# Polysketch attention and a noisy top-2 router on one core: reordering the head, summing early sketches in PSUM, and storing the last tiles together

## The chip, the cores and the metric

One core of a Trainium2 chip runs the whole kernel in one launch. The metric is device time in microseconds (us), the median of three runs: 346.47 before the change (346.46 to 346.67). Engines: PE is TensorE, DVE VectorE, ACT ScalarE, POOL GpSimd, SP SyncE. DMA transfers are issued by SP, ACT and POOL; "SPq" and "ACTq" in the profile are the issuing instructions.

## What is computed

Attention with sketched polynomial features for B=4 batches, H=4 heads, S=1088 positions, DH=32, R=8; its output, 4352 tokens of D=128, goes through a mixture of E=8 experts (F=1024) of which a noisy router takes two per token:

```python
def phi(x):                                   # R*R = 64 features per head
    a = einsum('rd,bhsd->bhsr', S1, x)
    b = einsum('rd,bhsd->bhsr', S2, x)
    return einsum('bhsi,bhsj->bhsij', a, b).reshape(..., 64)
q_p, k_p = phi(q), phi(k)
kv  = einsum('bhsf,bhsd->bhfd', k_p, v);  z = k_p.sum(axis=2)
attn = einsum('bhsf,bhfd->bhsd', q_p, kv) / (einsum('bhsf,bhf->bhs', q_p, z) + 1e-6)
x = attn.transpose(0, 2, 1, 3).reshape(4352, 128)
noisy = x @ w_gate + log1p(exp(x @ w_noise)) * noise
top2 of noisy per token, weights = softmax over the two
out[token] = sum over its two experts e of weight * (relu(x @ w1[e]) @ w2[e])
```

All inputs and the output are float32.

## The kernel before

**Planning.** No engine's order is written out by hand. Every piece of work is a job in a `Plan` with an engine (or a choice of two), an estimated cost, a priority (lower is sooner), what it reads and writes, and the rotating buffers it opens. The planner lists the jobs in time on its own cost figures; each engine then executes its instructions in exactly the planned order, waiting on semaphores where data come from another engine. A change in a cost or a priority can so move instructions that it does not mention.

**Head, batch 0.** A token tile is 128 positions; a batch has eight and a half tile. SP loads the sketch words, keys, values and queries. The sketch words are split into a high and a low part `s` (`split`, L555), turned by PE (L535/536) and copied by DVE to `sk` (L541), a matrix of 128 x 128 whose column halves are the high and the low part, so that the features are a sum of two products. `turned` (L583) transposes keys and queries on DVE (kT, qT). `features` (L595) multiplies a tile's kT or qT by `sk` in one matmul of 128 columns (L606), leaving the high and the low result side by side in PSUM; ACT or DVE copies the low half out (`lo`, L322), DVE adds it to the high half (`ab`, L614), and another DVE product (L628) makes the 64 features (phk, phq). `keys_values` (L636) then sums features times values over all tiles (L669; `vaug` is the values with a column of ones, four copies by ACT or POOL), folds the router's weights into the result (L690) and copies it to `kvw` in two halves by partitions, one for each pair of heads. `queries` turns phq (L717), multiplies it by kvw (L728), and divides (den, L757/758; lh L745), which gives the logits `lg` (L747).

**Router, `router`.** ACT makes softplus parts u, sp; POOL makes a (L869, L870) from the logits and multiplies by the noise (L873 to L875); DVE makes `noisy` (L888), top, the gates g, the mask mk; PE counts the places of a token in its expert (L934, L937), and pos, gm follow. The noise is one SP load (136 KB) into a buffer `x`, laid out by six small POOL copies (L400). POOL also makes, at the kernel's start, constants for later: the padding block `pad` (L488/489), the limits `reach` and `capt` (L494/496), token numbers `pid` (L500 to L507), which are copied to the gather records `xg` (L984).

**Experts.** The first blocks (u=0 to 3) are gathered straight from SBUF: `block` builds four one-hot matrices `o` (DVE compare, L1054; the fourth by ACT as Abs and Relu, L1047/1050), PE multiplies them with the tokens (L1060), ACT copies to bT, PE runs hp (L1108), ACT relu (L1116), PE acc (L1123). Later blocks come through DRAM: POOL scatters tokens with indirect DMAs (L809), SP loads xb. Results go to `pairs` in DRAM by POOL's scatters; `sums` loads both results of each token (pr), DVE adds them (L1179) and SP or ACT stores the tiles. While PE has nothing to do in the first 30 us, `idle` puts in filler matmuls on zeros (L1435).

**Early work.** Four q tiles of batch 0 (4 to 7) and four k tiles of batch 1 (0 to 3) have their features matmuls before the router (`early`, PSUM tag acc); their lo copies on ACT and adds on DVE come behind it, as the one-hots' data (`gone`) tell.

**Tail.** The last blocks do not go through `pairs`: `to_tokens` (L1255) multiplies their results by one-hots of the tokens and sums them in three PSUM banks `totals`, one for tiles (0,1), one for the half tile (4), one for tiles (2,3), in this order. `sums` adds each to the pair sum (L1186), and ACT issues three stores: tiles (0,1), the half tile, tiles (2,3).

## Time and profile before

| | us |
|---|---|
| median of three runs | 346.47 |
| profiled execution: its own time | 347.08 |
| profiled execution: span from the first to the last instruction | 345.1 |
| PE busy in the span | 336.2 (97%) |
| POOL, DVE, ACT busy | 232.1, 146.4, 136.4 |
| first expert matmul (L1108) starts | 27.47 |
| last pair of L1255 begins / last total (L1186) begins | 338.50 / 339.25 |

Times inside the execution are counted from the span's start. A row of a timeline gives start, length, engine, line, operation, out<-in and how many instructions were put together; the brackets hold the idle time of the engine before it and what ended it. A row of the chain of waits gives start, length, engine, tile and line. A row of waits gives who waited for whom, total, count and longest. The mean granted clock of PE was 0.994 of full speed.

### The profile page before, as it was taken

To read this page: it belongs to the slowest core of one execution; us is meant where nothing else is said; L and a number is where in the kernel's file an instruction comes from. 1 tells how busy PE (TensorE), PEld (TensorE's weight loads), DVE (VectorE), ACT (ScalarE), POOL (GpSimd) and SP (SyncE) were. 2 spreads that over 40 slices of the span, in tenths; PEclk is the share of its full clock that TensorE was granted. 3 is DMA by queue.
4 is the path that set the end of the run, shared out by engine and by line. 5 is a ranking of instruction groups with operands and counts; after the bars stand their busy time and mean duration, and the time that the engine had idled before them with its cause. 6 is when DMAs were issued, how large, how long until landed. Compare 5 with 4: busy or idle time off the path is not lost.

```text
span 345.1 us, 7493 instructions
## 1 busy us (share of the span) xinstructions
PE 336.2 (97%) x2585; PEld 313.9 (91%) x2586; DVE 146.4 (42%) x547; ACT 136.4 (40%) x305; POOL 232.1 (67%) x385
## 2 busy tenths in 40 slices
PE   8999999999999999999999999999999999999992
PEld 3859999999999999999999999999999999999992
DVE  5889794877636688555862000020102000112101
ACT  2357542543531445323334333433334333434430
POOL 8854868896899857898968889878334433354410
PEclk9999999999999999999999999999999999999997
DMA  7999839144571376511353213365125211114421
GB/s 217 327 346 268 288 63 356 60 116 114 139 221 39 62 187 133 138 40 39 74 74 71 54 43 54 69 184 120 37 36 185 67 32 27 29 32 166 147 77 39
DMA packets 68922, 41.17 MB, mean 119 GB/s; under 512 B 49877, under 2 KB 61078, under 8 KB 68880
## 3 DMA queue, kind: packets, MB, share of 16 engines
q1 hardware_dynamic: 63360, 30.93, 35.1%
q0 software_dynamic: 4704, 9.15, 8.2%
q10 hardware_dynamic: 816, 0.58, 0.6%
q8 instruction: 21, 0.34, 0.4%
q14 instruction: 21, 0.17, 0.2%
HBM read 24.18 MB, written 16.65 MB: 118 GB/s over the span
## 4 chain that ended last, share of the span: by engine, by line
PE 95%; DVE 2%; ACT 1%; issue 1%; POOL 0%; DVEq 0%; ACTq 0%; POOLq 0%
PE acc L1123 37%; PE hp L1108 37%; PE bank L606 5%; PE bank L728 4%; PE bank L669 4%; PE bank L717 2%; PE hp L1435 1%; PE acc L669 1%; PE bank L1255 1%; PE turn L1060 1%; PE bank L690 0%; ACT o L1050 0%; PE bank L937 0%; DVE lg L747 0%; ACT o L1047 0%
## 5 line engine op out<-in xcount | busy, mean ns | idle before, releaser
L1123 PEld LDWEIGHTS acc<-w2s,h 128*128 128x128 f32 x1152 | 145.8, 192 | 4.6
L1123 PE MATMUL acc<-w2s,h 128*128 128x128 f32 x1152 | 149.8, 275 | 0.0
L1108 PE MATMUL hp<-bT,w1s 128*128 128x128 f32 (+1 forms) x768 | 147.3, 328 | 0.2 <-ACT bT L322 0.2
L1116 ACT ACTIVATE h<-hp 128x512 f32<-128x512 f32 x144 | 86.0, 597 | 123.2 <-PE hp L1108 122.9
L1108 PEld LDWEIGHTS hp<-bT,w1s 128*128 128x128 f32 x768 | 111.6, 191 | 6.4 <-ACT h L1116 0.5
L809 POOL DMA_INDIRECT pairs<-y,ix x66 | 65.1, 986 | 66.1 <-ACT y L322 55.9
L809 POOL DMA_INDIRECT xs<-xg,to x72 | 73.0, 1014 | 19.2 <-issue 9.1
L808 POOL MEMSET zb<- 128x400 bf16 (+1 forms) x142 | 63.1, 444 | 0.2 <-PE hp L1435 0.2
L1096 DVE STREAM_TRANSPOSE bT<-xb 128x256 f32<-128x256 f32 (+1 forms) x40 | 15.6, 390 | 101.9 <-PE hp L1108 89.8
L322 ACT COPY y<-acc 128x128 f32<-128x128 f32 (+1 forms) x48 | 15.3, 320 | 28.1 <-PE acc L1123 27.6
L1179 DVE TENSOR_TENSOR o<-pr 128x512 f32<-128x512 f32 (+2 forms) x13 | 6.7, 525 | 36.1 <-DMA pr<-pairs 36.1
L728 PE MATMUL bank<-kvw,pT 128*128 128x98 f32 x144 | 18.2, 274 | 0.0
L728 PEld LDWEIGHTS bank<-kvw,pT 128*128 128x128 f32 x144 | 17.4, 192 | 0.6 <-DVE kvw L322 0.3
L669 PE MATMUL bank<-phk,vaug 128*128 128x128 f32 (+1 forms) x108 | 13.1, 277 | 0.0
L322 ACT COPY lo<-bank 128x256 f32<-128x256 f32 (+3 forms) x20 | 6.5, 328 | 16.5 <-PE bank L606 16.5
L322 ACT COPY pT<-bank 128x512 f32<-128x512 f32 (+1 forms) x16 | 8.8, 559 | 10.6 <-PE bank L717 9.1
L669 PEld LDWEIGHTS bank<-phk,vaug 128*128 128x128 f32 (+1 forms) x108 | 12.5, 191 | 0.4
L614 DVE TENSOR_TENSOR ab<-bank,lo 128x256 f32<-128x256 f32 (+3 forms) x20 | 7.2, 360 | 12.5 <-ACT lo L322 12.4
L628 DVE TENSOR_TENSOR phk<-ab 128x512 f32<-128x512 f32 (+1 forms) x20 | 12.2, 629 | 0.4
L628 DVE TENSOR_TENSOR phq<-ab 128x512 f32<-128x512 f32 (+1 forms) x20 | 11.8, 628 | 0.2
L991 DVE TENSOR_TENSOR xg<-x,g 128x512 f32<-128x512 f32 (+1 forms) x16 | 11.2, 750 | 0.0
L1435 PE MATMUL hp<-zb 128*128 128x512 bf16 x29 | 9.5, 463 | 1.6 <-DVE zb L439 1.3
(177 smaller groups left out, 243.7 us busy)
## 6 DMA issues: line engine op xcount, KB each, us to landing
xs<-pad SPq DMA_DIRECT2D x9, 516.0 KB
w1s<-in_moe_w_dram SPq DMA_DIRECT2D x8, 512.0 KB
w2s<-in_moe_w_dram SPq DMA_DIRECT2D x8, 512.0 KB
pr<-pairs SPq DMA_DIRECT2D x7, 512.0 KB
xb<-xs SPq DMA_DIRECT2D x96, 32.0 KB
kq<-in_k_dram SPq DMA_DIRECT2D x4, 544.0 KB
kq<-in_q_dram SPq DMA_DIRECT2D x4, 544.0 KB
vld<-in_v_dram SPq DMA_DIRECT2D x14, 128.0 KB
```

The source lines that it names most:

```text
L322: paces.append(A.copy(o, i) if e == "ACT" else V.tensor_copy(o, i))
L606: T.matmul(ps.t[rows, 2 * W * i:2 * W * i + 2 * W], lhsT=lhsT, rhs=sk[:].rearrange("p c h x -> p (c h x)"), start=True, stop=True)
L628: V.tensor_tensor(out=jobs[i][2].t[rows, jobs[i][1]:jobs[m - 1][1] + 1, :, :].rearrange("p c h (i j) -> p (c h) i j", i=R), in0=factors(i, ...
L669: T.matmul(kvp.t[:, P * a:P * a + P], lhsT=va.t[0:K, t, hs, :].rearrange("p h d -> p (h d)"), rhs=pk.t[0:K, t, hs, :].rearrange("p h f -> ...
L728: T.matmul(ps2.t[:, c0:c0 + 2 * YW], lhsT=pT.t[:, P * (2 * i + a):P * (2 * i + a) + P], rhs=kvw.t[:, a, :], start=True, stop=True)
L808: G.memset(zb[:, 0:FIRST_SPACER if kind == "first" else SPACER], 0.0)
L809: ins = G.indirect_dma_start(**kw)
L1096: add("DVE", vec(P * n), lambda _: V.transpose(bT.t[:, 0:P * n], flat()), r=[xb], w=[bT], prio=TOP + u)
L1108: T.matmul(hp.t[:, P * n * i:P * n * (i + 1)], lhsT=w1s[:, e, P * (js * g + i):P * (js * g + i + 1)], rhs=bT.t[:, 0:P * n], start=True, st ...
L1116: paces.append(A.activation(out=h.t[:], in_=hp.t[:], func=AF.Relu))
L1123: T.matmul(acc.t[:, D * c:D * c + D], lhsT=h.t[:, P * (n * i + c):P * (n * i + c + 1)], rhs=w2s[:, e, j, :], start=(j == 0 and c == 0), st ...
L1435: ins = T.matmul(warm()[:], lhsT=zb[:, 0:P], rhs=zb[:], start=True, stop=True)
```

## The change

In words, in the order of the diff:

1. `lo` is gone as a buffer; the low half is copied into `ab` (four buffers instead of two) and added in place.
2. Head keys: the first transpose (tiles 0, 1) gets priority -51, ahead of `sk` on DVE; the other key transposes follow at 0.5, 0.9 and 1.9, so that the four features groups of the keys stand together.
3. The value copies of the head get priority 2.05 and a POOL cost of 0.45; POOL's jobs of priority 13 and more (pad, limits, token numbers) depend on them. In the planned order POOL makes three of the four copies (two before), then wg, pad, the first limits, the noise copies, and only then the token numbers.
4. The two early features groups are `summed`: per tile two matmuls of 64 columns (high, then low) accumulate in the same PSUM columns, and one ACT copy behind the router's `sp` brings the sum to `ab`.
5. The two halves of `kvw` in the head are written by ACT and DVE, declared apart so that neither waits for the other; the early key transposes of batch 1 wait for both.
6. The fourth one-hot of block 0 is a DVE compare like the other three; blocks 1 to 3 keep ACT, at a cost of 0.45.
7. The tail: the last batch's four tiles are one piece with two loads and two pair sums; the totals lie in two banks, the half tile in one, both pairs of tiles in the other; PE's order is (4), (0,1), (2,3); SP stores the half tile and ACT all four tiles in one store.

```diff
     tag("qT", 1, [P, S])
-    tag("lo", 2, [P, 4, 2 * R * H])
-    tag("ab", 2, [P, 4 * H, 2, R])
+    tag("ab", 4, [P, 4 * H, 2, R])
     tag("kvT", 2, [P, 2, R * R])
...
             paces.append(A.copy(o, i) if e == "ACT" else V.tensor_copy(o, i))
+            return paces[-1]
...
     def pool_job(cost, prio, emit, w, r=()):
-        add("POOL", cost, lambda e: emit(), r=r, w=w, prio=prio)
+        job = add("POOL", cost, lambda e: emit(), r=r, w=w, prio=prio)
+        if prio >= 13:
+            behind_values.append(job)
+    behind_values = []
...
-    def features(jobs, prio, after=(), first=None, early=None):
+    def features(jobs, prio, after=(), first=None, early=None, summed=False):
...
                 lhsT = xT.t[:, P * t:min(P * t + P, S)]
+                if summed:
+                    for c in range(2):
+                        T.matmul(ps.t[rows, W * i:W * i + W], lhsT=lhsT, rhs=sk[:, c, :, :].rearrange("p h x -> p (h x)"),
+                                 start=(c == 0), stop=(c == 1))
+                    continue
                 T.matmul(ps.t[rows, 2 * W * i:2 * W * i + 2 * W], lhsT=lhsT,
                          rhs=sk[:].rearrange("p c h x -> p (c h x)"), start=True, stop=True)
-        last = (add if early is None else plan.add)("PE", n * mm(128), emit, lat=0.15, r=["sk"] + [(xT, t) for xT, t, _ in jobs],
+        last = (add if early is None else plan.add)("PE", n * (2 * mm(64) if summed else mm(128)), emit, lat=0.15, r=["sk"] + [(xT, t) for xT, t, _ in jobs],
                    w=[ps], prio=prio if first is None else first, touch=[dst for _, _, dst in jobs], after=after if early is None else (early,))
-        lo, ab = new("lo"), new("ab")
-        gone = [] if early is None else [onehot["pos"], onehot["gm"]]
+        ab = new("ab")
+        flat = lambda: ab.t[rows, 0:n * H, :, :].rearrange("p (i h) w r -> p i (h w r)", h=H)
         x4 = lambda: ps.t[rows, 0:2 * W * n].rearrange("p (i c y) -> p i c y", i=n, c=2)
-        add(EV, either(W * n), lambda e: copy(e, lo.t[rows, 0:n, :], x4()[:, :, 1, :]), r=[ps] + gone, w=[lo], prio=prio)
-        add("DVE", vec(W * n), lambda e: V.tensor_tensor(
-            out=ab.t[rows, 0:n * H, :, :].rearrange("p (i h) w r -> p i (h w r)", h=H),
-            in0=x4()[:, :, 0, :], in1=lo.t[rows, 0:n, :], op=ALU.add), r=[ps, lo], w=[ab], prio=prio if early is None else 12.95 if jobs[0][2] is kv_of[0][1] else 13.2)
+        if summed:
+            add("ACT", act(W * n), lambda e: copy(e, ab.t[rows, 0:n * H, :, :].rearrange("p x w r -> p (x w r)"), ps.t[rows, 0:W * n]),
+                r=[ps], w=[ab], prio=prio if early is None else 12, after=() if early is None else (onehot["sp"],))
+        else:
+            add(EV, either(W * n), lambda e: copy(e, flat(), x4()[:, :, 1, :]), r=[ps], w=[ab], prio=prio)
+            add("DVE", vec(W * n), lambda e: V.tensor_tensor(out=flat(), in0=x4()[:, :, 0, :], in1=flat(), op=ALU.add), r=[ps], w=[ab],
+                prio=prio)
...
     kv_of, behind_first, freed = {}, [], []
-    behind_gates = []
+    behind_gates, folded_first = [], []
...
         for h in range(H):
-            add(("ACT", "POOL") if head else "ACT", {"ACT": act(256), "POOL": 0.4} if head else act(256), lambda e, h=h: copy(e, va.t[:, 0:C, h, 0:DH], vld.t[:, h, 0:C, :]),
-                r=["ones_v"] + [(vld, l) for l in range(4)], w=[(va, h)], prio=prio + 2.2, after=hold)
+            value = add(("ACT", "POOL") if head else "ACT", {"ACT": act(256), "POOL": 0.45} if head else act(256),
+                        lambda e, h=h: copy(e, va.t[:, 0:C, h, 0:DH], vld.t[:, h, 0:C, :]),
+                        r=["ones_v"] + [(vld, l) for l in range(4)], w=[(va, h)], prio=prio + (2.05 if head else 2.2), after=hold)
+            if head:
+                for job in behind_values:
+                    job.deps.add(value)
         add("ACT", act(128), lambda e: A.copy(va.t[0:HB, C, :, 0:DH], vld.t[0:HB, :, C, :]),
...
             if early is not None and i == 0:
-                turned(kT, kld, c0, c1, 22, True)
-                features([(kT, t, pk) for t in range(c0, c1)], prio + i + 1, after, 21.5, early)
+                turned(kT, kld, c0, c1, 22, True).deps.update(folded_first)
+                features([(kT, t, pk) for t in range(c0, c1)], prio + i + 1, after, 21.5, early, True)
                 continue
-            freed.append(turned(kT, kld, c0, c1, prio + i))
+            freed.append(turned(kT, kld, c0, c1, (-51, 0.5, 0.9)[i] if head else prio + i))
             features([(kT, t, pk) for t in range(c0, c1)], prio + i + 1, after)
-        freed.append(turned(kT, kld, 8, 9, prio + 1))
+        freed.append(turned(kT, kld, 8, 9, prio + (1.9 if head else 1)))
         turned(qT, qld, 8, 9, prio + (25 if head else 2))
...
         for l in range(2):
-            add(EV, either(98), lambda e, l=l: copy(
-                e, kvw.t[64 * l:64 * l + 64, :, YW * l:YW * l + YW],
-                ps.t[64 * l:64 * l + 64, 0:2 * YW].rearrange("p (a y) -> p a y", a=2)),
-                r=[ps, "kvw0"], w=[(kvw, l)], prio=prio + 3)
+            def half(e, l=l):
+                ins = copy(e, kvw.t[64 * l:64 * l + 64, :, YW * l:YW * l + YW],
+                           ps.t[64 * l:64 * l + 64, 0:2 * YW].rearrange("p (a y) -> p a y", a=2))
+                if head:
+                    apart(ins, "kvw")
+                    wrote(ins, "kvw")
+            done = add(("ACT", "DVE")[l] if head else EV, 0.25 if head else either(98), half, r=[ps, "kvw0"], w=[(kvw, l)], prio=prio + 3)
+            if head:
+                folded_first.append(done)
         turned(qT, qld, 4, 8, prio + 5)
...
                 behind_first.append(features([(qT, C, pq)], prio + 26, (), 913))
-                features([(qT, t, pq) for t in range(4, 8)], prio + 26, (), prio + 11, early)
+                features([(qT, t, pq) for t in range(4, 8)], prio + 26, (), prio + 11, early, True)
             return rest
...
     pairs_t = pairs[:].rearrange("(t k) d -> t k d", k=2)
-    APART = "rows of other waves, or of other tokens"
+    APART = "rows of other waves, or of other tokens, or other columns"
     DATA = mybir.DependencyInfo(mybir.DependencyClass.Sync, mybir.DependencyReason.DATA)
...
         actf(0.25, lambda: A.activation(out=t3("u"), in_=t3("u"), func=AF.Exp), ["u"], ["u"])
-        actf(0.25, lambda: A.activation(out=t3("sp"), in_=t3("u"), func=AF.Ln, bias=1.0), ["u"], ["sp"])
+        soft = actf(0.25, lambda: A.activation(out=t3("sp"), in_=t3("u"), func=AF.Ln, bias=1.0), ["u"], ["sp"])
+        onehot.setdefault("sp", soft)
         def noise_of():
...
             for c in range(4):
-                if c == 3:
-                    add("ACT", act(P), lambda e_, c=c: A.activation(
+                if c == 3 and u:
+                    add("ACT", 0.45, lambda e_, c=c: A.activation(
                         out=oh.t[:, c, :], in_=place[:], func=AF.Abs, scale=-1.0, bias=onehot["pos"].t[:, c, e:e + 1]),
                         r=["place", onehot["pos"]], w=[(oh, c)], prio=(-900, 12.9, 14.5, 15.5)[u])
-                    add("ACT", act(P), lambda e_, c=c: A.activation(
+                    add("ACT", 0.45, lambda e_, c=c: A.activation(
                         out=oh.t[:, c, :], in_=oh.t[:, c, :], func=AF.Relu, scale=onehot["less"].t[:, e:e + 1],
...
                 wrote(ins, "read")
-            dma("SP", lambda t=t, rows=rows, cs=cs: t.t[rows, cs, :, :].rearrange("p c k d -> p (c k d)"), lambda src=src: src,
-                [key for w in range(last + 1) for key in results[w]], [(t, c0)], prio, size=1024.0 * c * rows.stop, done=done)
-            add("DVE", vec(P * c), lambda e, t=t, o=o, rows=rows, cs=cs: V.tensor_tensor(
-                out=o.t[rows, cs, :], in0=t.t[rows, cs, 0, :], in1=t.t[rows, cs, 1, :], op=ALU.add),
-                r=[(t, c0)], w=[(o, c0)], prio=prio)
+            n = 2 if b == B - 1 and c == 4 else c
+            for d in range(0, c, n):
+                ds = slice(c0 + d, c0 + d + n)
+                dma("SP", lambda t=t, rows=rows, ds=ds: t.t[rows, ds, :, :].rearrange("p c k d -> p (c k d)"),
+                    lambda src=src, d=d, n=n: src[..., 2 * D * d:2 * D * (d + n)],
+                    [key for w in range(last + 1) for key in results[w]], [(t, ds.start)], prio, size=1024.0 * n * rows.stop, done=done)
+                add("DVE", vec(P * n), lambda e, t=t, o=o, rows=rows, ds=ds: V.tensor_tensor(
+                    out=o.t[rows, ds, :], in0=t.t[rows, ds, 0, :], in1=t.t[rows, ds, 1, :], op=ALU.add),
+                    r=[(t, ds.start)], w=[(o, ds.start)], prio=prio)
             if last == NW:
                 tot = totals[at]
-                def more(e, o=o, tot=tot, rows=rows, cs=cs):
-                    V.tensor_tensor(out=o.t[rows, cs, :], in0=o.t[rows, cs, :],
-                                    in1=tot.t[rows, 0:P * (cs.stop - cs.start)].rearrange("p (c d) -> p c d", d=D), op=ALU.add)
-                add("DVE", vec(P * c), more, r=[tot, (o, c0)], w=[(o, c0)], prio=prio)
-            dma(queue, lambda dst=dst: dst, lambda o=o, rows=rows, cs=cs: o.t[rows, cs, :].rearrange("p c d -> p (c d)"), [(o, c0)],
+                for k in (range(1, 3) if c > 1 else (0,)):
+                    def more(e, o=o, tot=tot, rows=rows, cs=cs, k=k):
+                        ks = slice(2 * k - 2, 2 * k) if k else cs
+                        V.tensor_tensor(out=o.t[rows, ks, :], in0=o.t[rows, ks, :],
+                                        in1=tot.t[rows, P * ks.start:P * ks.stop].rearrange("p (c d) -> p c d", d=D), op=ALU.add)
+                    add("DVE", vec(P * min(c, 2)), more, r=[(tot, k)], w=[(o, c0 + (2 * k - 2 if k else 0))], prio=prio)
+            dma(queue, lambda dst=dst: dst, lambda o=o, rows=rows, cs=cs: o.t[rows, cs, :].rearrange("p c d -> p (c d)"), [(o, c0 + d) for d in range(0, c, n)],
                 [("out", (b, at))], prio, size=512.0 * c * rows.stop)
...
         if not totals:
-            totals.extend(new("bank") for _ in range(3))
+            totals.extend(new("bank") for _ in range(2))
         at, oh = new("den"), new("kq")
...
         add("DVE", 0.3 + vec(512 + HB), ones_of, r=[ix, tokens["t"]], w=[at, oh], prio=p_last)
-        for k, cols in enumerate(((0, 1), (4,), (2, 3))):
+        for k, cols in enumerate(((4,), (0, 1), (2, 3))):
             def emit(_, k=k, cols=cols):
-                for i, c in enumerate(cols):
+                for c in cols:
                     M = HB if c == 4 else P
-                    T.matmul(totals[k].t[0:M, D * i:D * i + D], lhsT=oh.t[:, P * c:P * c + M], rhs=y.t[:, 0:D],
-                             start=(e == E - LAST and i == 0), stop=(e == E - 1), skip_group_check=True)
-            add("PE", len(cols) * mm(D), emit, lat=0.15, r=[oh, y], w=[totals[k]], prio=prio + k)
+                    T.matmul(totals[min(k, 1)].t[0:M, D * (c % 4):D * (c % 4) + D], lhsT=oh.t[:, P * c:P * c + M], rhs=y.t[:, 0:D],
+                             start=(e == E - LAST and c in (0, 4)), stop=(e == E - 1), skip_group_check=True)
+            add("PE", len(cols) * mm(D), emit, lat=0.15, r=[oh, y], w=[(totals[min(k, 1)], k)], prio=prio + k)
     p_last = 399
...
             sums(B - 1, part_of(B - 1, [(0, 4)]), w, 901)
-    pieces = part_of(B - 1, [(4, 2), (6, 2)], True)
-    sums(B - 1, [pieces[0], pieces[2], pieces[1]], NW, 902, ("ACT",))
+    pieces = part_of(B - 1, [(4, 4)], True)
+    sums(B - 1, [pieces[1], pieces[0]], NW, 902, ("SP", "ACT"))
```

## The prediction

> **What bounds the kernel now.** I read the page first: PE is busy for 97% of the span and holds 95% of the chain that ended last; its row in the 40 slices is full from the second slice to the last but one, and the granted clock with it.
>
> ```profile
> PE 336.2 (97%) x2585; PEld 313.9 (91%) x2586; DVE 146.4 (42%) x547; ACT 136.4 (40%) x305; POOL 232.1 (67%) x385
> PE   8999999999999999999999999999999999999992
> PEclk9999999999999999999999999999999999999997
> PE 95%; DVE 2%; ACT 1%; issue 1%; POOL 0%; DVEq 0%; ACTq 0%; POOLq 0%
> ```
>
> From the first expert matmul (L1108, 27.47) to the last (L1123, about 337) PE has no work taken away by this change, and its gaps in that stretch sum to about 1 us. So the end is the time at which that first L1108 runs, plus a fixed body, plus the tail after the last L1123. The change is worth what it does to these two ends. The chain of waits over the first 45 us shows what sets the start:
>
> ```profile
> 6.44 0.36 DVE kT L590
> 6.85 2.11 PE bank L606 x14
> 8.96 0.54 PE hp L1435 x2
> ...
> 19.87 0.39 DVE lg L747
> 20.33 0.36 POOL a L869
> ...
> 26.99 0.26 ACT lo L322
> 27.25 0.17 ACT bT L322
> 27.47 2.05 PE hp L1108 x16
> ```
>
> The attention logits (lg) of the first batch, then the router on POOL and DVE, then one-hots, gather (L1060), the ACT copy bT. The reader should see that POOL stands in it only from 20.33. The timeline of POOL shows how near it is to standing there sooner:
>
> ```profile
> 7.33 0.96 POOL L488 MEMSET pad<- 128x1032 f32 x1
> 8.35 0.16 POOL L489 IOTA pad<- 128x8 int32 x1
> 8.52 1.00 POOL L320 COPY vaug<-vld 128x256 f32<-128x256 f32 x2
> 9.82 1.75 POOL L464 COPY wg<-wst 32x16 f32<-32x16 f32 x4 [0.30 <-DMA wst<-in_moe_w_noise_dram]
> ...
> 12.46 0.16 POOL L500 MEMSET pid<- 128x72 int32 x1
> ...
> 14.75 2.29 POOL L400 COPY noise<-x 32x256 f32<-32x256 f32 x6
> 17.10 0.20 POOL L984 COPY xg<-pid 128x8 int32<-128x8 int32 x1
> ...
> 20.33 0.35 POOL L869 TENSOR_SCALAR a<-lg 128x32 f32<-128x32 f32 x1 [0.54 <-DVE lg L747]
> ```
>
> The queue is full from 9.82 to 19.79; its slack before a, the wait for lg, is 0.54 us. The noise copies at 14.75 wait for nothing: the pid numbers ahead of them (12.46 to 14.75) covered the landing of the noise load, which SP issued at 7.82 and which the trace marks as landed at 14.35.
>
> **Change, POOL's queue (the step that decides).** In the changed program's order POOL does: three value copies, wg, the pad memset and iota, reach/capt, then the noise copies, only then pid, then xg and limits, then a. The pad, limits and pid are tied behind the value copies, and the noise copies have been planned ahead of pid. Sum, all durations from the rows above: wg still waits for its load, so 9.82 + 1.75 = 11.57; pad with its iota took 7.33 to 8.51, 1.18, to 12.75; reach/capt took 11.65 to 12.46, 0.81, to 13.6. The noise copies now stand before 14.35 and wait about 0.8 us with everything behind them. Then 14.35 + 2.35 (14.75 to 17.10) = 16.7; pid 2.29 to 19.0; xg, nine limit operations and xg again took 17.10 to 19.79, 2.69, to 21.7; a at about **21.75, 1.4 later than 20.33**. Of the 1.4, 0.8 is the wait, the rest is the pad and the third value copy that moved behind the front of the queue, less the 0.54 of slack. SP's order up to the noise load is unchanged, so 14.35 should hold. Its ends: 13.9 and 14.8, and limits at 0.2 or 0.3 us each: a is 0.9 to 1.9 later.
>
> **Head of the attention.** Keys had landed at about 5.6 (SP waited 2.1 us for them until then); kT can run at 5.62 instead of 6.44, in the 0.60 us in which DVE waited for the sketch's transposes. The first L606 then follows sk, ended 6.44, at 6.54 instead of 6.85: 0.31 won. The two fillers at 8.96 go (0.54), but the value sums L669 then need the four value copies, of which POOL makes three: at most 0.5 is won. The kvw halves:
>
> ```profile
> DVE kvw L322 <- ACT kvw L322: 1.0, 1, 1.0
> ```
>
> DVE's half stood at 16.58 behind ACT's (16.32 to 16.55); side by side L728 starts at about 16.75, where PE comes free, not 16.90: 0.15. So lg comes 0.35 to 0.85 sooner, at 19.4 to 19.9. All of it lies beside POOL's queue, which ends at 21.7: it is worth nothing unless POOL is quicker.
>
> **Summed sketches.** The early features (four q tiles, four k tiles) turn 8 matmuls of 128 columns into 16 of 64. Here a rule speaks for and the row against: the Trainium skill, "TensorE: Matmul & The Clock Gate", section on the back-to-back issue gap, prices a matmul by its columns, so 64 cost half of 128 and the sum stays what it was, about 1.8 us for the two groups as at 18.76 and 19.68 (1.06 each with the first's latency). The nearest row is L728, 98 columns:
>
> ```profile
> 16.90 2.03 PE L728 MATMUL bank<-kvw,pT 128*128 128x98 f32 x16
> ```
>
> 16 records in 1.79 us net of the last one's latency, 0.112 each, just what 128 columns take: these f32 matmuls run at the rate of their weight loads (PEld 192 ns mean, overlapped). By the row each group doubles, +1.8 us in all; I take the row. Either way it is free: the matmuls run from about 18.1 to 22, where PE otherwise runs fillers (20.79 to 25.3), and nobody needs their PSUM until ACT copies it after sp. In return two lo copies and two adds of ab go from the stretch before the first expert matmul.
>
> **From router to first L1108.** From a to the gather the chain is the old one. The fourth one-hot of block 0 moves from ACT (Abs and Relu, 26.50 + 0.49) to DVE (a seventh compare), and the lo copy no longer stands before bT. The gather ended at 26.87, bT ran at 27.25: now it follows the gather at once, and L1108 would be at 27.20 but for POOL: 0.27 won. With POOL: 27.47 + 1.4 - 0.27 = **28.6, +1.1** (ends +0.6 and +1.6). PE's sequence behind it shows no new long wait: the scatters, xb loads and weights are due later by their old rows, and all the rest moves along.
>
> **Tail.** Now one pass for the half tile, then tiles (0,1), then (2,3), stored by SP (half) and ACT (four tiles). Before:
>
> ```profile
> 337.50 1.72 PE L1255 MATMUL bank<-y,kq 128*128 128x128 f32 x10 [0.35 <-ACT y L322]
> 338.25 0.64 DVE L1186 TENSOR_TENSOR o<-o,bank 128x256 f32<-128x256 f32 x2 [0.95 <-PE bank L1255]
> ...
> 338.70 3.04 ACTq L338 DMA_DIRECT2D out_dram<-o  x3
> 339.25 0.42 DVE L1186 TENSOR_TENSOR o<-o,bank 128x256 f32<-128x256 f32 x1 [0.36 <-PE bank L1255]
> ```
>
> ACT issued three stores one after the other until 341.74, the last landed at 343.27 and SP closed 1.7 us later. After: both pairs of tiles lie in one PSUM bank, and in the built program PE's first matmul of (2,3) waits for DVE's total of (0,1); on PE nothing stands behind it but the rest of (2,3), on DVE only the last total. (4) and (0,1) end at 338.57, DVE 338.61 to 339.03, (2,3) 339.09 to 339.80, DVE to 340.26 (before 339.67, so +0.6), issue at 340.29. The same store of 256 KB, 324.77 to 327.21, needed 2.44: landed 342.73, **0.5 won** (ends 0.3 and 0.9, as other such stores took 2.04 to 2.36). The two pair loads instead of one piece each lie in the 10 us that DVE idles there.
>
> **Sum.** +1.1 - 0.55 = about +0.6. The profiled execution (347.08, span 345.1) would become 347.7; it is 0.61 above the median of 346.47, so the median becomes **347.1**.
>
> **Rivals.**
> - *POOL does not bind* (faster). If the noise lands by about 12.6, or POOL's small copies run closer, a follows lg, which is 0.35 to 0.85 sooner, say 0.6; with 0.27 behind the gather and 0.5 of the tail: 1.35 won, **345.1**. For it: the noise is only 136 KB and its first piece was marked at 12.14. Against: its last piece at 14.35, behind the w2s load on the same queue. Chance 0.13.
> - *PE's clock drops in the longer wait* (slower). The same page, section on the clock gate, says that PE falls to half rate after an idle window of some 3.4 us and needs as long to return. The row: the first nine fillers (1.27, 4.02 us for nine) took 0.43 us each, later ones 0.22, so a cold PE is seen here. After the change PE has two fillers left between the summed features (ended about 22.1) and top (about 24.5): some 2.0 to 2.3 us idle. By the rule nothing happens below 3.4; above it the first four us of L1108 run at half, +2.1: **349.2**. It decides from a wait 1.2 us longer than reckoned, or a shorter window than the page gives. Chance 0.12.
> - *The tail saves all* (no change). If the wait in the shared bank costs nothing, DVE ends at 339.43, the store lands at 341.9: 1.4 won, **346.2**. Against it is the order of the two instructions. Chance 0.05.
>
> **How the numbers follow.** Forecast 0.70, its own range 346.5 to 347.9 from POOL's ends (+0.6 to +1.6), the tail's and 0.3 of gaps in the body. What a measurement can tell is 0.2%, 0.69 us: from 345.78 to 347.16 is no change, and the forecast lies just inside its upper edge; half of it, 0.36, goes to slower. With the clock: slower 0.48. Faster: 0.13. The same: 0.39. Range 345.6 to 348.3: it takes in most of POOL's rival and the upper end of the forecast, and leaves out the clock's.
>
> **What would show it.** Right: POOL's row of noise copies carries an idle before it released by the noise load, with pid behind, a near 21.8, and DVE's noisy waiting for POOL; the first L1108 near 28.6; the summed L606 at 0.11 us a record; L728 and lg earlier than before; in the tail L1255 in two groups with an idle released by DVE between, one ACT store, landed 2.4 us after issue. Wrong: a with its idle released by lg (then POOL's rival), L1108 spaced at twice 0.11 (the clock), or a new idle of PE between 30 and 335.

## The result and the profile after

The changed kernel took **350.55 us** (349.31 to 351.16, six runs) against 346.63 for the kernel before on the same chip: ratio 1.0107 (95% interval 1.0087 to 1.0126). It is slower by 3.9 us; 347.1 was forecast. Its profiled execution took 350.54, its span is 348.4, so the traces differ by 3.4. First the page after: busy times, slices, granted clock, and the chain that ended last by engine.

```profile
PE 337.2 (97%) x2593; PEld 315.6 (91%) x2594; DVE 148.3 (43%) x551; ACT 133.9 (38%) x298; POOL 232.0 (67%) x386
PE   8979999999999999999999999999999999999992
PEclk9998999999999999999999999999999999999998
PE 84%; POOL 6%; DMA 5%; DVE 2%; issue 1%; SPq 0%; ACT 0%; POOLq 0%
```

PE is as busy as before, but it holds 84% of the chain instead of 95%, POOL and DMA 11%. One digit of the clock, in the slice from 26 to 35 us, has fallen to 8. The chain of waits of the first 50 us (start, length, engine, tile, line) says what took PE's place:

```profile
7.95 6.52 DMA x<-in_moe_noise_dram
14.53 0.39 POOL noise L400
...
21.87 0.35 POOL a L891
...
30.24 1.39 POOL xs L830
...
33.64 3.40 POOL xs L830
...
46.39 3.44 DMA xb<-xs
49.88 0.33 PE turn L1106
```

Before, the chain went to PE for good at 27.47. Now it runs from the noise load over POOL to a, and on over POOL's scatters (L830) to PE's first token tile that comes through DRAM (xb), at 49.88. The third scatter took 3.40 us; before it took 1.36.

How far PE stands behind the same work of before, in these two executions: 1.75 at the first expert matmul (29.22 against 27.47), 1.5 at 46, 2.5 behind the wait for xb, 3.2 from 112 on, 3.2 at ACT's last copy of y (340.36 against 337.18), 3.4 at the end. The other 0.5 of the 3.9 is not in these traces: the profiled execution of before (347.08) was 0.45 slower than its median.

**The start.** POOL's timeline (start, length, line, operation, in brackets the idle time before it and its releaser):

```profile
14.53 2.19 POOL L400 COPY noise<-x 32x256 f32<-32x256 f32 x6 [1.51 <-DMA x<-in_moe_noise_dram]
...
21.87 0.35 POOL L891 TENSOR_SCALAR a<-lg 128x32 f32<-128x32 f32 x1
```

The noise copies wait, and a has no idle before it: POOL's own queue decides it, 1.54 later than before. Then PE's timeline and, in the second fence, stretches of the same time (length, busy time and instructions of PE, PEld, DVE, ACT and POOL, then the granted clock, the share of the DMA engines and GB/s):

```profile
19.82 1.84 PE L612 MATMUL acc<-sk,kT 128*128 128x64 f32 x15
21.71 0.59 PE L1462 MATMUL hp<-zb 128*128 128x512 bf16 x2
24.24 1.57 PE L1462 MATMUL hp<-zb 128*128 128x512 bf16 x6 [1.93 <-DVE top L918]
...
26.68 2.05 PE L1082 MATMUL turn<-o,x 128*128 128x128 f32 x8
```

```profile
24.00:26.00 2.00, 1.76 (x12) 0.74 (x13) 1.82 (x18) 1.58 (x9) 0.45 (x2) 0.92 1.17 289
26.00:27.00 1.00, 1.00 (x3) 0.35 (x2) 0.96 (x5) 0.71 (x3) 0.39 (x2) 0.50 1.19 151
27.00:28.00 1.00, 1.00 (x6) 1.00 (x6) 1.00 (x6) 0.23 (x1) 0.32 (x1) 0.50 1.11 187
28.00:29.00 1.00, 1.00 (x6) 0.73 (x5) 0.86 (x6) 0.23 (x2) 0.00 (x0) 0.50 1.17 238
```

PE has nothing for 1.93 us, starts again at 24.24, and from 25.70 to 29.11 its clock is granted at half: the gather L1082 takes 2.05 us. In the runs below where the clock stayed up (e5 and e11 with the same queue and a pause of 1.4 to 1.5, e2 with the pause filled) it takes 1.25, and a to the first expert matmul takes 6.41 us in all three, here 7.35. The clock costs 0.94 here.

The length of the pause alone does not decide it. In e3 PE paused longer, for 2.10, the clock stayed at 1.00 throughout, and a to the first expert matmul took 6.41 again:

```profile
24.79 1.57 PE L1476 MATMUL hp<-zb 128*128 128x512 bf16 x6 [2.10 <-DVE top L932]
```

The clock that each trace records shows what does. It changes in steps only: the half clock here lasted 3.41 us, and each full stretch that ends in a change, in all seventeen traces, is a whole number of steps of 3.413 us (20.48, 317.44, 334.51, 337.92 or 341.33). Those stretches hold 1,682 steps. Behind 18 of them the clock fell to half, seventeen times at a kernel's end; each of the 18 has in all 1.70 us or more without a matmul, and each of the others 1.45 at most. Here the pause lies whole within one step, from 22.29 to 25.70, which has 1.93 idle. In e3 a step ends at 23.77, inside the pause: the step before has 1.07 idle, the one behind 1.28. In these traces the steps begin at another instant of each execution (the first full one at 4.1 to 7.3), so the same pause can halve the clock in one execution and leave it in the next.

**The third scatter.** DVE's timeline before, then after:

```profile
32.51 1.28 DVE L628 TENSOR_TENSOR phq<-ab 128x512 f32<-128x512 f32 x2
33.83 0.22 DVE L614 TENSOR_TENSOR ab<-bank,lo 64x64 f32<-64x64 f32 x1
34.08 0.42 DVE L628 TENSOR_TENSOR phq<-ab 64x256 f32<-64x256 f32 x1
34.42 1.28 DVE L628 TENSOR_TENSOR phk<-ab 128x512 f32<-128x512 f32 x2
```

```profile
33.13 0.20 DVE L627 TENSOR_TENSOR ab<-bank,ab 64x64 f32<-64x64 f32 x1
33.37 1.62 DVE L640 TENSOR_TENSOR phq<-ab 64x256 f32<-64x256 f32 x3
34.91 1.28 DVE L640 TENSOR_TENSOR phk<-ab 128x512 f32<-128x512 f32 x2
```

And POOL's third scatter, before and after:

```profile
33.27 1.36 POOL L809 DMA_INDIRECT xs<-xg,to  x1 [0.17 <-issue]
...
33.64 3.40 POOL L830 DMA_INDIRECT xs<-xg,to  x1 [0.16 <-issue]
```

After, five products with both operands in SBUF follow each other without a break from 33.37 to 36.19. Before, the add of the half tile's ab, with one operand in PSUM, stood between the second and the third of them. That add is not one of those that went to PE: these two ran at 27.28 and 30.36, ahead of all five products. It was only planned elsewhere, at 33.13, ahead of the whole row; which edit made the planner do so was not tested. The scatter ends 0.84 us after the end of the row of products that it meets: at 34.63 before (the row ends at 33.80), at 37.03 after (36.19). The same 0.84 stands in all seventeen traces, whether the scatter took 1.36 or 3.40.

The delay reaches PE through POOL's queue. Before, POOL issued the load of xb at

```profile
44.41 2.22 POOL L338 DMA_DIRECT2D xb<-xs  x4 [1.97 <-DMA xs<-xg,to]
```

and PE took xb at 47.88 without a wait. After, the issue is at 46.39 and PE waits for xb until 49.88.

**In the middle** PE's transposes of phq (L738) take turns with ACT's copy of their PSUM bank:

```profile
107.08 0.66 PE L738 MATMUL bank<-ident,phq 128*128 128x128 f32 x4
108.41 0.66 PE L738 MATMUL bank<-ident,phq 128*128 128x128 f32 x4 [0.68 <-ACT pT L321]
```

Before, all eight ran in one piece, and the fold behind them (L690) had 0.24 of idle:

```profile
106.28 1.09 PE L717 MATMUL bank<-ident,phq 128*128 128x128 f32 x8
107.61 0.44 PE L690 MATMUL bank<-wg,kvT 33*64 33x49 f32 x8 [0.24 <-ACT pT L322]
```

**The tail**:

```profile
340.68 1.07 PE L1282 MATMUL bank<-y,kq 128*64 128x128 f32 x6 [0.35 <-ACT y L321]
...
341.79 0.42 DVE L1213 TENSOR_TENSOR o<-o,bank 128x256 f32<-128x256 f32 x1 [0.36 <-PE bank L1282]
...
342.26 0.71 PE L1282 MATMUL bank<-y,kq 128*128 128x128 f32 x4 [0.51 <-DVE o L1213]
343.01 0.42 DVE L1213 TENSOR_TENSOR o<-o,bank 128x256 f32<-128x256 f32 x1 [0.80 <-PE bank L1282]
343.47 0.67 ACTq L338 DMA_DIRECT2D out_dram<-o  x1
```

The pause of PE in the shared bank is there as forecast, and the store is issued as forecast. But its last piece landed at 346.64, 3.17 us after the issue, not 2.44; 14 of its 16 pieces had landed by 2.49.

### The profile page after: what moved, and what is told of

Its sections match the earlier page's. It is cut to its first block, busy times and chain, and to the rows that moved or that the text cites. A ratio compares the mean times of both kernels' runs of the same rounds, so it can differ in the third digit from the quotient of the medians.

```text
span 348.4 us, 7500 instructions
## 1 busy us (share of the span) xinstructions
PE 337.2 (97%) x2593; PEld 315.6 (91%) x2594; DVE 148.3 (43%) x551; ACT 133.9 (38%) x298; POOL 232.0 (67%) x386
## 4 chain that ended last, share of the span: by engine, by line
PE 84%; POOL 6%; DMA 5%; DVE 2%; issue 1%; SPq 0%; ACT 0%; POOLq 0%
PE acc L1145 36%; PE hp L1130 34%; PE bank L685 4%; PE bank L749 3%; PE bank L615 3%; POOL xs L830 3%; PE bank L738 2%; DMA x<-in_moe_noise_dram 2%; DMA vld<-in_v_dram 2%; DMA xb<-xs 1%; PE bank L1282 1%; POOL zb L829 1%; DMA xs<-xg,to 1%; POOL noise L400 1%; DVE o L1076 1%
## 5 line engine op out<-in xcount | busy, mean ns | idle before, releaser
L830 POOL DMA_INDIRECT pairs<-y,ix x66 | 65.5, 992 | 64.3 <-ACT y L321 50.8
L830 POOL DMA_INDIRECT xs<-xg,to x72 | 73.7, 1024 | 19.9 <-issue 8.9
L321 ACT COPY ab<-bank 128x256 f32<-128x256 f32 (+3 forms) x18 | 6.0, 334 | 14.0 <-PE bank L615 11.1
L738 PE MATMUL bank<-ident,phq 128*128 128x128 f32 x72 | 10.6, 277 | 0.7 <-ACT pT L321 0.7
L1462 PE MATMUL hp<-zb 128*128 128x512 bf16 x21 | 7.8, 511 | 3.3 <-DVE top L918 1.9
```

The costliest lines, as they stand in the source:

```text
L321: paces.append(A.copy(o, i) if e == "ACT" else V.tensor_copy(o, i))
L738: T.transpose(ps.t[:, c0:c0 + P], pq.t[:, t + i, 2 * a:2 * a + 2, :].rearrange("p h f -> p (h f)"), ident[:])
L830: ins = G.indirect_dma_start(**kw)
```

## Experiments

Each kernel below ran beside the kernel before on the same chip (medians of before 346.57 to 347.06); "over before" and the ratios are against that. Moves of order were written as a step on the planned order that takes marked jobs out and puts them in elsewhere:

```diff
-        for j in self.order():
+        order = self.order()
+        moved(order)
+        for j in order:
```

### POOL's queue

**e1**: noise copies moved behind the pid numbers, nothing else: `late = of("noise"); at = order.index(of("pid")[-1]) + 1`.

> The changed kernel (350.55 us, first expert matmul at 29.22, first tile that comes through DRAM used at 49.88) with one move: the six noise copies stand behind the token numbers on POOL, as before the change; every other engine's order is the same. Theory A (two chains: POOL's queue sets the router's start and through it both PE's start and POOL's scatters, whose tiles PE needs at 49.88): no wait for the noise load, a on POOL at about 20.4 instead of 21.87, PE's pause before top shorter than 1 us, so no drop of its clock; first expert matmul at about 27.3; the scatters start 1.5 us sooner, so the first tile from DRAM about 48.4: 1.5 us faster, about 349.0. Theory B (only PE's start counts, the pause at 49 is an accident of its own): 1.9 us faster or more, about 348.6 or less. Theory C (the wait for the noise was covered anyway): unchanged, 350.5.

348.96 (348.68 to 349.28), ratio 1.0057 (1.0044 to 1.0070): +1.9 over before. a at 20.30, first expert matmul 26.71, third scatter still 2.98. Half of the loss is this one order. It was not all of what the start had won: PE lost 1.66 us at 44.3 in a wait that is taken up below.

**e8**: the kernel *before* with only the noise copies moved ahead of pid.

> The kernel before the change, with one move only: POOL's six noise copies stand ahead of the token numbers, as in the changed kernel. Theory A: they wait for the noise load until about 14.4 and push everything behind them: a at 21.4 to 21.8 instead of 20.33, first expert matmul at 28.4 to 28.8, PE's clock stays up because PE has fillers there; 1.0 to 1.4 us slower than before. Theory C (the queue has enough slack): no slower than 0.2 us.

348.07 (347.75 to 348.88), ratio 1.0042 (1.0028 to 1.0057): +1.5. Noise waits 1.25, a at 22.00, first expert matmul 28.65, and the 1.18 it then lacks stay to the last accumulation. One line of POOL's order, put into the old kernel, makes it slower by over a third of the whole loss.

**e6**: the value copies no longer hold POOL's constants back, all replanned:

```diff
-                for job in behind_values:
-                    job.deps.add(value)
+                pass
```

> The changed kernel without the dependence of POOL's later constants (pad, limits, token numbers) on the value copies; the plan is made anew, and POOL's order up to the router is then that of before, noise behind the token numbers. Theory A: as with the noise copies moved alone (1.9 us over before), a at about 20.3, no half clock, first expert matmul below 27; the plan at 107 us is then also that of before, where PE waits 0.5 us less: 1.4 us over before, 348.0 to 348.4. Theory B (POOL's order is of no weight for the end): as the changed kernel, 350.5.

348.22 (347.75 to 348.73), ratio 1.0043 (1.0029 to 1.0058). a at 19.34, first expert matmul 26.33, 1.14 *sooner* than before; the third scatter again 3.24. The wait of L738 at 107 is gone in this plan (0.24 at the fold, as before), but PE falls back by 1.0 us between 120 and 180, and the tail has a store that needs 3.58. So the start's gain is real and is lost behind it.

### The pause and the clock

**e2**: eight more fillers in the pause (`if k == 0 and len(pieces) > 1: n += 8`). **e3**: the kT transpose that DVE made behind the products is put between the phq and the phk products. **e4**: both.

> The changed kernel with eight more filler matmuls on zeros in PE's pause of 2.1 us before top, so that PE does not stand still; nothing else is changed. If the clock fell to half because of that pause, the granted clock stays at 1.0 from 26 to 29 and the first expert matmul comes at about 28.3 instead of 29.22. Theory A (the first tile from DRAM is set by POOL's scatters, not by PE): that 1 us is lost again in a longer wait of PE for that tile at 49 (0.8 becomes 1.8), and the time stays within 0.3 us of 350.55. Theory B (one chain, through PE's start): 0.9 to 1.0 us faster, 349.6. Theory C (the clock falls for another reason than the pause): clock and start unchanged.

> The changed kernel with one move on DVE: the transpose of the next keys (kT, 0.70 us, one operand) stands between the three products phq and the two products phk, which otherwise follow each other without a gap from 33.4 to 36.2. Theory A (the third scatter of POOL took 3.40 us instead of 0.96 because POOL cannot get at SBUF while DVE runs products with two operands from SBUF back to back): the scatter gets through at the transpose, takes about 1.5 us, POOL's later scatters and the first tile from DRAM come 1.5 to 2 us sooner, the wait of 0.8 at 49 goes, and the kernel is 0.8 us faster, 349.75. Theory D (the scatter was held up by the pad stores that SP issues at 31.8 to 35.0): it still takes over 3 us, and the time is unchanged.

> Both edits: the fillers in PE's pause and the transpose between the products. Theory A (two chains that meet at the first tile from DRAM, each of which hides a gain in the other): 1.6 to 1.9 us faster than the changed kernel, 348.7 to 348.9, more than the sum of the two alone (0 and 0.8). Theory B (independent losses): the sum of what the two gave alone.

| | us | ratio | first expert matmul | third scatter | PE reaches xb |
|---|---|---|---|---|---|
| e2 | 349.99 | 1.0094 (1.0078 to 1.0111) | 28.28 | 2.97 | 49.23 |
| e3 | 349.62 | 1.0072 (1.0059 to 1.0085) | 28.84 | 1.77 | 49.07 |
| e4 | 349.37 | 1.0071 (1.0057 to 1.0084) | 28.05 | 1.77 | 47.97 |

With fillers (e2) the clock stays up and the first expert matmul comes 0.94 sooner, as worked out, but the time falls by 0.56 alone, between the two theories. In its trace PE loses 0.9 again at 45.08, in a wait for ACT that is taken up below; and since xb is ready only at 49.23, PE would have lost it there without that wait. e3 gains 0.9 to 1.2 us (by the medians, by the ratios) where 0.8 was expected. e4 gains no more than e3, where theory A asked for more than the sum of the two: what the fillers give is not seen beside the transpose. e3's DVE and POOL rows are

```profile
33.50 1.62 DVE L650 TENSOR_TENSOR phq<-ab 64x256 f32<-64x256 f32 x3
35.05 0.70 DVE L604 STREAM_TRANSPOSE kT<-kq 128x512 f32<-128x512 f32 x1
35.67 1.24 DVE L650 TENSOR_TENSOR phk<-ab 128x512 f32<-128x512 f32 x2
```

```profile
34.19 1.77 POOL L844 DMA_INDIRECT xs<-xg,to  x1 [0.17 <-issue]
35.96 0.34 POOL L843 MEMSET zb<- 128x280 bf16 x1
36.47 1.29 POOL L844 DMA_INDIRECT xs<-xg,to  x1 [0.17 <-issue]
```

and the scatter gets through at the transpose: 1.77 and 1.29 for the two, instead of 3.40 and 0.96; it ends 0.84 us after the end of the last phq (35.12). Theory D, the pad stores, would have left it over 3. Of the scatters in the trace of before that met no DVE operation with two inputs in SBUF (107 of 142) the longest took 1.08. The Trainium skill, "SBUF — State Buffer", in its account of the shared port pair, says that a DVE operation with two SBUF inputs and a GpSimd operation that reads SBUF exclude each other, the second waiting for the first to end. The rows agree, and add that the scatter can lose the pair several times over to instructions that follow closely. The page infers further that TENSOR_TENSOR leaves the making of DMA descriptors alone; the scatters of this case were held up all the same.

**e7**: e6, with the limits behind the router's sp, the transpose between, and three banks (below).

> The changed kernel with every loss found so far taken out: no dependence of POOL's constants on the value copies, the later limits behind the router's POOL work, the keys' transpose between the products phq and phk, three PSUM banks for the totals. Theory A: a follows lg at about 19.5 to 20, first expert matmul at 26.0 to 26.5 (before 27.47), the first tile from DRAM at 47 or sooner, the tail 0.5 us shorter than before: 1.3 us faster than before the change, 345.2 to 345.6. Rival F (something else holds the body behind 40 us, as ACT's late copy of y in the run with the noise moved): level with before, 346.3 to 347.

348.07 (347.61 to 349.06), ratio 1.0042 (1.0026 to 1.0059): a miss. The limits moved behind sp now stood ahead of POOL's part of the gates, so the first expert matmul came at 27.57 with a at 19.91. The waits of e6 from 120 on stayed.

**e9**: the change's own plan with moves alone: noise behind pid, the limits behind `less`, the transpose between, three banks.

> The changed kernel with moves of order alone: POOL's noise copies behind pid, the limits behind the router's copy of less, the kT transpose between the two groups of DVE products, and the totals of the last tiles in three banks. Theory (the loss is two chains at the start, POOL's queue up to a and the slowed third scatter): a at 19.5 to 20.0, first expert matmul 25.9 to 26.4 (before 27.47), third scatter about 1.8 us, PE's first use of a tile from DRAM at 46.5 or sooner, the 0.5 at 107 stays, tail -0.5 to 0: about 1 us faster than before, ratio 0.997. Rival (something else in the body takes the gain, as ACT's late y at 44 in the run with noise behind pid): last accumulation where it was, level with before, ratio 1.000 to 1.003.

347.33 (346.56 to 348.06, 22 runs), ratio 1.0009 (1.0000 to 1.0017). Three orders on POOL and DVE and a bank take the loss back to nearly nothing. Its profile starts 0.8 ahead and is level with before from 112 on (it loses 0.46 at 47 in the wait for xb and 0.6 around 105, where PE waits 0.68 for ACT's copy): of the two expectations the rival's came true.

### The tail

**e5**: three banks instead of two (`totals.extend(new("bank") for _ in range(3))`, each pair of tiles in its own). **e10**: the kernel before with the change's tail alone. **e12**: e10 with the four tiles in two stores, tiles 0 and 1 by SP. **e13**: e10 with both stores by ACT, `sums(..., NW, 902, ("ACT",))`. **e14**: e13 with three banks. **e15**: e9 with both stores by ACT.

> The changed kernel with the totals in three PSUM banks again, one for the half tile and one for each pair of tiles; orders and stores stay as changed. Theory A (PE's 0.7 us pause in the last matmuls is a wait for DVE because both pairs lie in one bank, and the end hangs on it): the pause goes, the last total and the store's issue come 0.6 us sooner, and the kernel is 0.6 us faster than the changed one, so 3.3 us slower than before instead of 3.9. Theory E (the end is set by the landing of the one large store, whatever its issue): within 0.2 us of the changed kernel.

> The kernel before with the tail of the change alone (half tile first, one pass of four tiles, two banks, one store of ACT). Theory (the last store lands slowly, 2.9 to 3.5 us, when it is alone in flight): tail 8.3 to 8.8 against 8.2, so +0.1 to +0.7 over before, ratio 1.0003 to 1.002. The prediction's own step: -0.55, ratio 0.998.

> The kernel before with the tail of the change, but the four tiles leave in two stores, tiles 0 and 1 by SP as soon as their total stands and tiles 2 and 3 by ACT. Theory (the pieces that come late are those in flight while the engines fetch the code behind the last branch, some 1 us behind the store's issue): the same fetch meets the last store again, 14 of its 16 pieces by 2.3, the last at 2.8 to 3.2, tail about 8.0 to 8.4, level with before. Rival (the size of the store makes the late pieces): with half the bytes the last store lands in 2.1 to 2.3, tail about 7.5, ratio 0.998.

> The kernel before with the tail of the change, two banks, but both stores go out by ACT, so that SyncE has no work behind its loads of the pairs. Theory (the half tile's store by SyncE holds SyncE's last branch back until the end, and its code fetch of 2.7 us then lies across the only store): SyncE branches near 335 and is back near 338, one fetch of 1.1 us fewer behind the store's issue at 340.2, the store's last piece at 2.45 to 2.7 instead of 3.25, tail 7.6 to 7.9 against 8.46 with SyncE's store, so 0.3 to 0.6 less than before, ratio 0.998 to 0.9995. Rival (a store of four tiles has late pieces by itself): 3.2 again, tail 8.4, ratio 1.000 to 1.0015.

> The same with the totals in three banks, so that TensorE does not pause for VectorE in between. Theory: the store is issued 0.4 to 0.5 earlier, tail 7.2 to 7.5, ratio 0.997 to 0.998. Rival: the pause goes but late pieces eat it, tail 8.0, ratio 1.000.

> The run of moves alone (noise behind pid, limits late, kT between the products, three banks) with both last stores by ACT. Theory: its last accumulation stays where it was (0.0 to 0.3 after before's), its tail falls from 7.94 to 7.3 or 7.5, so 0.5 to 0.8 faster than before, ratio 0.998. Rival (the body gives the start's gain away in most executions, by the bank wait at 105 and ACT's late results near 44): ratio 1.000 to 1.002.

The trace also records SP's and PE's branch behind their last work, and code being fetched, a packet of 16 KB on queue 8 that starts 1.1 to 1.6 us after PE's last branch in every run. "Tail" is from ACT's last copy of y to the end.

| | ratio | PE's branch | packet | last store issued | its last piece | SP's branch, next | tail |
|---|---|---|---|---|---|---|---|
| before | | 338.15 | 339.2-340.6 | 341.04 | 2.23 | 335.03, 337.75 | 7.88 |
| after | 1.0107 | 342.94 | 344.0-345.1 | 343.47 | 3.17 | 342.98, 345.74 | 8.07 |
| e10 | 1.0034 (1.0023 to 1.0045) | 339.68 | 340.8-341.7 | 340.19 | 3.25 | 339.70, 342.32 | 8.15 |
| e12 | 1.0049 (1.0030 to 1.0067) | 340.31 | 341.5-342.4 | 340.84 | 2.73 | 341.31, 344.18 | 8.68 |
| e13 | 1.0024 (1.0011 to 1.0038) | 339.55 | 341.2-342.1 | 340.15 | 3.42 | 334.88, 337.63 | 8.31 |
| e5 | 1.0062 (1.0048 to 1.0077) | 339.77 | 340.9-342.1 | 341.14 | 2.93 | 341.43, 343.93 | 7.35 |
| e14 | 0.9992 (0.9980 to 1.0005) | 338.10 | 339.2-340.4 | 339.46 | 2.86 | 334.96, 337.94 | 6.97 |
| e15 | 0.9995 (0.9983 to 1.0007) | 339.16 | 340.2-341.6 | 340.53 | 2.84 | 336.03, 339.00 | 6.95 |

Three banks alone take 1.5 us off the changed kernel (e5: 348.95, 348.18 to 349.37) where 0.6 was expected; 0.7 of it is in the tail of its profile, and the clock stayed up in it as well. The tail alone makes the old kernel slower (e10), so the forecast 0.55 won was a loss. By the medians it is 1.2 us, more than e10's own theory had. Its profiled execution, the quickest of its 22, shows 0.27 of that in the tail; where the rest lies stays open. e12 was expected level with before and is slower. That SP's late branch delays the store's pieces fell with e13: SP is free at 337.63 and the last piece needs 3.42. What SP does cost is seen in e12: SP does nothing for 2.9 us after its branch, its own waits come only then, and the end stands 2.84 behind the landing. It is 1.79 in the others of this table, where SP was back in time, and 2.09 in e5, where SP was back 0.14 before the landing. The Trainium skill, "Runtime: NRT & Kernel Launch", on instruction fetch, says that a taken branch out of the loaded pages stalls the engine for a fetch from memory; SP's 2.5 to 3.0 us from branch to next instruction in this table would be its size here, but no run tells the fetch from another cause.

The late pieces go with code packets, PE's above all. Queues in the store's flight of e13, then of e14 (packets, MB, share of 16 engines' time):

```profile
q10 hardware_dynamic: 144, 0.26, 20.6%
q8 instruction: 1, 0.02, 1.7%
q14 instruction: 2, 0.02, 1.1%
```

```profile
q10 hardware_dynamic: 224, 0.30, 29.1%
q14 instruction: 2, 0.02, 1.8%
```

1.7% of 16 engines over 3.5 us is 0.95 us on one engine. With two banks PE's pause puts its branch so late that this packet falls behind the store's issue, and ends 1.5 to 2.1 us after it, when the store's data, which begin to move 1.2 to 1.3 after the issue, are on their way (last piece at 3.17 to 3.62 in nine runs, and at 2.73 in e12 with half the bytes). With three it starts ahead of the issue and is over before the data move (2.84 to 3.06 in five). In the old tail, with 128 KB in the last store, ACT's first two stores held that one back, and the packet is over at its issue (2.23, and 2.08 in e8). That the packet is the cause is read from this order; it was not taken away by itself, and the two packets of 8 KB on queue 14 fall into both flights, so part of the lateness may be theirs. The price of the bank is shown: e14 against e13 is 1.3 us of tail, 0.8 of them at the issue.

**e14 has the lowest median of the kernels with changes**: the old kernel with the new tail in three banks and no store by SP, 346.48 (346.11 to 348.36), level with before within its interval. Its tail of 6.97 is shorter than forecast, but the ratio of 0.997 to 0.998 was not reached. e15 puts the mended tail on the mended start and is level too, where 0.998 was forecast. No kernel here is shown to be faster than before.

### The change once more

> The changed kernel once more, beside the others of this call. Theory: ratio 1.009 to 1.012; first expert matmul 28.3 (clock kept) to 29.3 (clock halved), third scatter 2.5 to 3.5, last store's last piece 3.0 to 3.6 with 14 of 16 pieces by 2.5.

350.71 (350.09 to 350.99), ratio 1.0103 (1.0079 to 1.0127). Here PE's pause was 1.40 and the clock stayed up; the first expert matmul came at 27.85, 1.4 sooner than in the first profile, and the time is the same. ACT's and PE's timelines show the largest of the places where it went:

```profile
43.28 0.27 ACT L321 COPY y<-acc 128x128 f32<-128x128 f32 x1 [3.30 <-PE hp L1130]
```

```profile
39.41 1.95 PE L1145 MATMUL acc<-w2s,h 128*128 128x128 f32 x16
...
44.76 1.49 PE L1145 MATMUL acc<-w2s,h 128*128 128x128 f32 x11 [0.72 <-ACT h L1138]
```

The acc that y copies ended at 41.36 by the records; ACT got its signal some 1.9 us later, and PE then lost 1.0 in its wait for ACT's h. The same is in e1 (1.66), e2 (0.89) and e15 (0.87), and smaller in e12 (0.33), whose order there is the old one. Its cause stays open.

## Why the prediction was wrong

- **POOL's queue: right.** Noise wait, pid behind it, a at 21.87 for 21.75. e1 and e8 show from both sides that this order carries the start.
- **Head and summed sketches: right.** L612 with 64 columns runs at 0.112 us a record (16 in 1.95 less the last one's latency), as the row of L728 said and not half of it. The section on the back-to-back issue gap, which the prediction names, gives its rule by columns for a matmul by itself; for a stream of weight loads and matmuls, it says, both set the spacing, and the rows of this case are such a stream. All of it lay under POOL's queue.
- **"From router to first L1108", +1.1: mis-sized.** a to the first expert matmul took 0.73 less than before where 0.27 was taken, and the clock 0.94 more where nothing was: +1.75.
- **The clock, a rival at 0.12: came true in the profiled execution.** The pause was forecast well (2.0 to 2.3; 1.93 to the first wait for top). The rule's 3.4 us of idleness was trusted over that: here 1.93 was enough, while 1.40, 1.49 and e3's 2.10 were not, since what counted was the idle time within one step of 3.41. (The page that the prediction names calls its window free-running, and the traces agree; it asks for an idle window, and 1.70 of 3.41 was enough.) It cost 0.94 of the forecast +2.1 at the first expert matmul. What it costs at the end is not settled: e2 without it is 0.56 faster than the changed kernel; of the result's six executions the two with a mean clock of 0.995 took 349.31 and 349.76, the four with 0.990 to 0.992 took 350.54 to 351.16; but e11's five, all with 0.993 or more, took 350.09 to 350.99.
- **"PE's sequence behind it shows no new long wait": the step that failed.** It took the scatters and the xb loads at their old rows, moved along, and did not look at what DVE would run beside them: the new plan took the half tile's add from between the two-operand products. A scatter of 1.36 became 3.40, xb was issued 2.0 us later behind the row of scatters, and PE lost 0.9 at 49.88. The rest of this step is the wait at 108, made by the replanning: PE falls behind by another 0.6 between 95 and 112.
- **Tail: the landing was mis-sized.** Every instant up to the issue was forecast (340.29 relative to before; 343.47 less 3.2). The 2.44 was taken from a store in mid-kernel; the last store, with code packets in its flight, took 3.17, in e11 3.62. The loss is +0.19, not -0.55.

Together: 1.75, less 0.2 regained by 46, plus 0.9 at xb, plus 0.7 more up to 112, plus 0.19: 3.4.

## What to carry to other kernels

When a plan is made anew, ask of each operation that moves what it kept apart: a VectorE add of 0.22 us between products was what let GpSimd's scatter through. Work moved ahead of a load's landing blocks the whole in-order queue behind it, so a queue with half a microsecond of slack is to be reckoned first and alone. A last store is priced by last stores, and a PSUM bank that two pairs of tiles share was paid for twice at the end here, with 0.8 us at the store's issue and 0.6 in its landing (e14 against e13).

## What was not expected of the hardware

- Five VectorE products with two SBUF inputs in a row stretched an indirect DMA's issue on GpSimd from 1.36 to 3.40 us; one transpose among them brought it to 1.77. In every trace it ended 0.84 us after the row of products that it met.
- TensorE's clock went by steps of 3.41 us: it fell to half behind each step with 1.70 us or more without a matmul, and behind none with 1.45 or less. So a pause of 1.93 halved it, about 1.5 us after work had come again, and one of 2.10 across two steps did not.
- A 16 KB code packet of about 1 us lies on one DMA engine; in its company 1 or 2 of a store's 16 pieces came 0.5 to 1.1 us behind the rest.
- SyncE took 2.5 to 3.0 us from its last branch to its next instruction; VectorE and ScalarE 0.2 to 0.6.
